# A fused RWKV attention, Fourier mixing and MLP kernel: another written-out order of the same operations, and an empty GpSimd instruction behind the transfers that GpSimd issues

## The chip, the core and the metric

The kernel runs on one core of a Trainium2 chip. The metric is the device time of one execution in microseconds (us); three runs of the kernel before gave 171.8, 172.41 and 172.97, so the median is 172.41 us. The engines are PE (TensorE, the matrix engine), DVE (VectorE), ACT (ScalarE), POOL (GpSimd) and SP (SyncE, which here only issues transfers). Each engine runs its own instructions strictly in the order in which the program lists them.

## The reference

Inputs are r, k and v of shape (4, 8, 768, 48): 4 batches, 8 heads, 768 steps, 48 channels a head; w and u of shape (8, 48); and two MLP weights, 384 x 1536 and 1536 x 384. All are float32, as is the output (4, 768, 384).

```
for t in range(768):                       # linear attention with decay w and bonus u
    cur   = u*k[t] (outer) v[t]
    y[t]  = r[t] @ (state + cur)
    state = w*state + k[t] (outer) v[t]
x   = y with the 8 heads side by side      # (4, 768, 384)
mix = real(fft over 768 steps of fft over 384 channels of x)
u2  = x + mix
un  = (u2 - mean) / sqrt(var + 1e-6)       # over the 384 channels
out = u2 + relu(un @ w_ch1) @ w_ch2
```

## The kernel before, in words

The 768 steps of each batch are cut into 6 chunks of 128, so there are 24 chunks, numbered 0 to 23 (0 to 5 are batch 0). For each chunk:

- `load` fetches k, r and v (192 KB each) through SP's queue (three of chunk 0 through ACT's) into rings of 6 buffers.
- `attend` scales k and r by powers of w into KR (L397, L400; DVE or POOL), transposes KR on PE (L421) and copies the result to KRT (L431 ACT, L432 DVE), or lets a DMA transpose it (L427). It multiplies KRT's halves into PR (L443, L445), makes the scores on PE (L455), masks them into MA (DVE straight from PSUM, L467; or an ACT copy AC, L462, and then POOL, L464), updates the state (L486, L499, L501), spreads the bonus into TT (L534), and sums the output X of the chunk (L546, L554, L556).
- `narrow` (batch 0, chunk by chunk) and `fold` (batches 1 to 3) add and subtract halves of X into HH and XF (L569, L572, L578 for batch 0). `fourier` does the two transforms as matmuls with tables (L647, L688), with TT and TR between them (L655, L656, L666, L669), adds x (UF, L700, L703), normalises (UB, L707 to L712; `st`, L718 or L719; `rstd`, L753), and transposes UB into UNT either on PE (L732, copied by L738 or L739) or by DMA (L758).
- `mlp1` and `mlp2` are the two MLP layers for each half batch (L776 with the ReLU in L781 or L782; L797 with L807). The outputs leave through POOL (L810) or SP (L811); the last 128 rows are cut in two (`finish`, L823 to L833).

Each output row block of 128 is worked on as soon as its inputs are there, so attention of later batches runs beside the MLP of earlier ones. The first MLP matmuls are those of half batch 1 (rows 384 to 767 of batch 0); what is written hp/1/ft below is layer 1 of that half, block ft. They need all three UNT blocks of that half and W1, which POOL fetches in two transfers of 576 KB (L851), called W1/0 and W1/1.

What sets the order is no loop. All operations are registered with a number, and with alternatives (which engine does it, or which way); the string `ORDER` lists some 1,410 of them as `number` or `number.alternative`, and `_Schedule.emit` emits them in this order. Buffers of a ring are handed out in it too. An engine's queue is thus the list's own operations in the list's order. `IDLES` registers matmuls on zeros (L283, `idle`), and `still` (L377) others; the list takes some of them.

POOL has one rule of its own, `chain`: each of its compute instructions carries a wait on the semaphore of the compute instruction before it. Transfers that POOL issues are outside the chain.

Of the kernel before, what the change touches and what calls it, by code (L numbers as in the profile page):

```python
# [61 lines left out]
class _Schedule:  # L62


    def __init__(self):
        self.ops, self.rings = [], {}
# [8 lines left out]
    def emit(self, order):  # L75
        last = {}
# [5 lines left out]
        for k, (n, a) in enumerate(order):  # L82
            o = self.ops[n]
            for t in o["new"]:
                ends = held[t.ring]
                m = min(range(len(ends)), key=ends.__getitem__)
                assert ends[m] < k, (o["name"], t.ring)
                ends[m] = last[t]
                t.value = self.rings[t.ring][m] if t.view is None else t.view(self.rings[t.ring][m])
            eng, key, fn = o["alts"][a]  # L90
            if fn is not None:
                made = fn()
                if eng == "POOL" and not key.startswith("dma"):
                    self.chain(made)
# [77 lines left out]
def kernel(  # L172
# [11 lines left out]
    nc = tc.nc  # L184
# [5 lines left out]
    hid_c = nc.inline_tensor(hid_n, name="hid_c")  # L190

    sch = _Schedule()
    before = []

    def chain(made):
        if before:
# [696 lines left out]
```

## Time and profile before

| what | value |
|---|---|
| runs (three) | 171.8, 172.41, 172.97 us |
| the profiled execution's own time | 173.32 us |
| its span, first to last instruction | 171.6 us |
| PE, DVE, ACT, POOL busy | 156.2, 127.8, 109.7, 92.3 us |
| instructions | 4305 |
| bytes moved by DMA | 27.08 MB, mean 158 GB/s |

The span is what the rows cover; 1.72 us of the execution lie around it. Busy times are unions of an engine's instructions. An engine that follows PE closely can be busy most of the time and yet wait for nothing that matters, so the stretches have to be read apart.

### The profile page before, as it was taken

To read this page: it belongs to the slowest core of one execution; us is meant where nothing else is said; L and a number is where in the kernel's file an instruction comes from. 1 tells how busy PE (TensorE), PEld (TensorE's weight loads), DVE (VectorE), ACT (ScalarE), POOL (GpSimd) and SP (SyncE) were. 2 spreads that over 40 slices of the span, in tenths; PEclk is the share of its full clock that TensorE was granted. 3 is DMA by queue.
4 is the path that set the end of the run, shared out by engine and by line. 5 is a ranking of instruction groups with operands and counts; after the bars stand their busy time and mean duration, and the time that the engine had idled before them with its cause. 6 is when DMAs were issued, how large, how long until landed. Compare 5 with 4: busy or idle time off the path is not lost.

```text
span 171.6 us, 4305 instructions
## 1 busy us (share of the span) xinstructions
PE 156.2 (91%) x1591; PEld 111.5 (65%) x1591; DVE 127.8 (74%) x310; ACT 109.7 (64%) x259; POOL 92.3 (54%) x128
## 2 busy tenths in 40 slices
PE   6179588999699999999999999999999999999991
PEld 1058466878477666867767687667766876766670
DVE  5298999899678959897867978988986984532241
ACT  2767898879578885765595676978634454562400
POOL 7548687799658142989774036578965221000021
PEclk9999978999999999999999999999999999999998
DMA  5999999899898999999989989999210217300223
GB/s 116 209 209 199 194 217 254 195 166 203 165 205 155 199 171 149 236 169 160 250 154 252 208 175 232 238 155 259 79 48 0 104 43 132 138 4 0 92 81 102
DMA packets 97879, 27.08 MB, mean 158 GB/s; under 512 B 94370, under 2 KB 96547, under 8 KB 97859
## 3 DMA queue, kind: packets, MB, share of 16 engines
q1 hardware_dynamic: 92480, 21.11, 68.4%
q0 software_dynamic: 2256, 5.12, 12.6%
q10 hardware_dynamic: 3122, 0.59, 2.1%
q8 instruction: 12, 0.20, 0.5%
q14 instruction: 9, 0.07, 0.1%
HBM read 19.77 MB, written 4.72 MB: 143 GB/s over the span
## 4 chain that ended last, share of the span: by engine, by line
PE 58%; DMA 12%; POOL 11%; DVE 6%; issue 6%; ACT 4%; POOLq 0%; DVEq 0%; ACTq 0%
PE bank L776 24%; PE bank L797 21%; DMA W<-in_moe_w_ch_dram 6%; POOL KR L397 3%; DMA wuc<-in_w_dram 3%; DMA KRT<-KR 3%; PE bank L647 2%; PE bank L688 2%; PE bank L455 2%; POOL MA L464 2%; PE bank L546 2%; POOL UB L712 1%; DVE TT L534 1%; PE bank L823 1%; POOL PR L443 1%
## 5 line engine op out<-in xcount | busy, mean ns | idle before, releaser
L776 PE MATMUL bank<-UNT,W 128*128 128x384 bf16 x288 | 54.3, 326 | 1.7 <-DMA W<-in_moe_w_ch_dram 1.3
L797 PE MATMUL bank<-W,HT 128*128 128x384 bf16 x276 | 52.3, 326 | 0.0
L781 ACT ACTIVATE HT<-bank 128x384 bf16<-128x384 f32 x73 | 33.1, 495 | 29.0 <-PE bank L776 28.8
L776 PEld LDWEIGHTS <-W 128*128 128x128 bf16 x288 | 31.1, 114 | 14.2 <-DMA W<-in_moe_w_ch_dram 1.5
L797 PEld LDWEIGHTS <-HT 128*128 128x128 bf16 x276 | 25.5, 97 | 14.2
L464 POOL TENSOR_SCALAR_AFFINE_SELECT MA<-AC 128x512 bf16<-128x512 bf16 x31 | 21.4, 690 | 14.3 <-issue 6.9
L810 POOL DMA_DIRECT2D out_dram<-osb x14 | 8.0, 571 | 28.2 <-DVE rstd L753 18.1
L397 POOL TENSOR_TENSOR KR<-kr,wtab 128x384 bf16<-128x384 f32 x17 | 19.1, 1124 | 6.8 <-ACT wtab L337 4.1
L462 ACT CAST AC<-bank 128x512 bf16<-128x512 f32 x31 | 17.7, 593 | 6.2 <-PE bank L455 2.8
L807 DVE SCALAR_TENSOR_TENSOR osb<-bank,rstd,UF 128x384 f32<-128x384 f32 x23 | 13.6, 612 | 7.8 <-PE bank L797 7.7
L782 DVE TENSOR_SCALAR HT<-bank 128x384 bf16<-128x384 f32 x23 | 12.3, 551 | 7.9 <-PE bank L776 5.9
L397 DVE TENSOR_TENSOR KR<-kr,wtab 128x384 bf16<-128x384 f32 x25 | 17.0, 697 | 1.3 <-DMA kr<-in_r_dram 1.3
L421 PE MATMUL bank<-ident,KR 128*128 128x128 bf16 x112 | 11.7, 252 | 4.8 <-DVE KR L400 3.7
L719 ACT ACTIVATE tn_t<-UF,sm 128x384 bf16<-128x384 f32 x21 | 13.1, 623 | 1.2 <-DVE UF L700 1.1
L421 PEld LDWEIGHTS <-KR 128*128 128x128 bf16 x112 | 8.8, 113 | 7.5 <-DVE KR L400 4.9
L534 DVE TENSOR_TENSOR TT<-V,bank 128x384 bf16<-128x384 bf16 x21 | 11.4, 548 | 2.7 <-ACT AC L462 1.2
L455 PE MATMUL bank<-KRT 64*128 64x128 bf16 x192 | 10.2, 229 | 2.0 <-ACT KRT L431 0.6
L554 DVE TENSOR_TENSOR X<-bank,TT 128x384 bf16<-128x384 f32 x17 | 9.2, 552 | 3.7 <-PE bank L546 3.6
L467 DVE TENSOR_TENSOR MA<-bank,mtri 128x512 bf16<-128x512 f32 x17 | 11.4, 682 | 0.6 <-PE bank L455 0.6
L647 PE MATMUL bank<-te_t,XF 128*128 128x193 bf16 x108 | 11.7, 247 | 0.0
L443 POOL TENSOR_TENSOR PR<-KRT 128x512 bf16<-128x512 bf16 x9 | 10.4, 1155 | 1.7 <-DMA KRT<-KR 1.1
L700 DVE SCALAR_TENSOR_TENSOR UF<-bank,X 128x384 f32<-128x384 f32 x21 | 11.0, 549 | 0.1
(112 smaller groups left out, 258.1 us busy)
## 6 DMA issues: line engine op xcount, KB each, us to landing
kr<-in_k_dram SPq DMA_DIRECT2D x23, 192.0 KB, 4.0
kr<-in_r_dram SPq DMA_DIRECT2D x23, 192.0 KB, 4.2
vt<-in_v_dram SPq DMA_DIRECT2D x23, 192.0 KB, 4.1
out_dram<-osb POOLq DMA_DIRECT2D x14, 192.0 KB, 3.3
out_dram<-osb SPq DMA_DIRECT2D x9, 192.0 KB, 2.6
W<-in_moe_w_ch_dram POOLq DMA_DIRECT2D x2, 576.0 KB, 9.2
W<-in_moe_w_ch_dram POOLq DMA_DIRECT2D x3, 384.0 KB, 7.1
te_t<-te_c SPq DMA_DIRECT2D x1, 579.0 KB, 5.0
```

Source lines behind the costliest of these rows:

```text
L397: return eng.tensor_tensor(out=o, in0=x, in1=y, op=AluOp.mult)
L421: nc.tensor.transpose(tps[s]()[:, p, :], KR()[:, s, p, :], ident)
L455: nc.tensor.matmul(A_ps[a]()[:, p, :], lhsT=KRT()[rows, 0, p, :], rhs=QT(p, rows), start=(p == 0), stop=(p == NP - 1), skip_group_check=True)
L462: op(("AC", i, a), [("ACT", "AC", lambda: nc.scalar.copy(AC(), A_ps[a]())), ("NONE", "", None)], r=[("A", i)], w=[("AC", i, a)], new=[AC], ...
L464: op(("MA", i, a), [("POOL", "MA", lambda: nc.gpsimd.affine_select(out=MA[a](), in_=AC(), pattern=[[0, NP], [1, 128]], base=0, channel_mul ...
L534: return eng.tensor_tensor(out=TT(), in0=V(), in1=x.unsqueeze(2).to_broadcast([128, H, D]), op=AluOp.mult)
L647: nc.tensor.matmul(fp()[:, par, :], lhsT=lhsT[:, g * CH:g * CH + 128], rhs=rhs, start=(nb == 0 and par == 0), stop=(nb == last and par == ...
L719: ("ACT", "SQ", lambda: nc.scalar.activation(out=squares, in_=UF()[:, j, :], func=Act.Square, scale=-float(DM), bias=sm()[:, j:j + 1], acc ...
L776: nc.tensor.matmul(hp(), lhsT=W1[:, dt, ft // 4 * 512 + ft % 4:(ft // 4 + 1) * 512:4], rhs=UNT()[:, :, dt, :], start=(dt == 0), stop=(dt = ...
L781: op(("HT", hf, ft), [("ACT", "HT", lambda: nc.scalar.activation(out=HT()[:, ft, :], in_=hp(), func=Act.Relu, scale=-1.0)), ("DVE", "HT", ...
L797: nc.tensor.matmul(mo(), lhsT=HT()[:, ft, j * 128:(j + 1) * 128], rhs=W2[:, ft, :], start=(ft == 0), stop=(ft == 11))
L807: one(("osb", hf, j), "DVE", "osb", lambda: nc.vector.scalar_tensor_tensor(out=osb(), in0=mo(), scalar=rstd()[:, j:j + 1], in1=UF()[:, j, ...
```

## The change

It is made of two parts.

First, `ORDER` is another list. It holds 1,414 entries of the same registered operations (before 1,413). Apart from the idle matmuls the operations are the same; their order and many of their alternatives differ. Decoded, the kinds that move most, by engine, with before -> after:

| kind (line) | DVE | POOL | ACT |
|---|---|---|---|
| scale k or r alone (L397) | 25 -> 26 | 17 -> 12 | |
| scale both at once (L400) | 3 -> 5 | | |
| PR (L443; L445 from PSUM) | 10 -> 15; 5 -> 3 | 9 -> 6 | |
| MA (L467; L464 with AC, L462) | 17 -> 22 | 31 -> 26 | 31 -> 26 |
| TT (L534; with DE, L530) | 21 -> 17 | 3 -> 7 | 3 -> 7 |
| KRT copies (L431, L432) | 13 -> 11 | | 15 -> 17 |
| HH, batch 0 (L569; L572 from PSUM) | 7 -> 4; 2 -> 6 | 3 -> 2 | |
| XF, batch 0 (L578) | 7 -> 11 | 5 -> 1 | |
| HH, other batches (L605) | 10 -> 12 | 2 -> 0 | |
| TR (L666, L669) | 2 -> 4 | 3 -> 1 | 3 -> 3 |
| UF (L700, L703) | 21 -> 23 | | 3 -> 1 |
| UB (L709, L712, L707) | 2 -> 4 | 11 -> 9 | 11 -> 11 |
| variance (L718 + L724; L719) | 3 -> 0 | | 21 -> 24 |
| ReLU of layer 1 (L782, L781) | 23 -> 27 | | 73 -> 69 |
| outputs issued (L810; SP: 11 -> 9) | | 14 -> 16 | |

On PE the idle matmuls go from 7 of 512 columns and 3 of 384 to 5 and 6, and matmuls that add x (L697) from 3 to 1. The DMA transposes stay 10 for KRT and 7 for UNT.

Places in the two lists that the prediction speaks of:

- W1 on POOL's queue. Before: the steps of XF for chunks 3 and 5 with W1/0 (1308) and W1/1 (1309) between them, then the rest. After: HH of chunk 5 (478.1), W1/1, PR of chunk 7 (522), W1/0, then V of chunk 8. PR of chunk 7 needs the copy KRT/7/1 (521), which is on DVE's queue.
- UNT of half batch 1: before two of its three copies from PSUM are DVE's (1080.3 and 1084.3), after one (1082.2).
- SP's queue behind r of chunk 12. Before: v/8, k/10, k/11, r/11, r/10, v/9, v/10, k/15 and then the transposing transfer UNT/0/0 (1057.4). After: UNT/0/0 stands right behind r/12, and v/10, k/15, k/13, k/11, r/11 and more behind it.
- ACT's second table load, `sqrttab` (192): before between X of chunk 2 and S of chunk 5, in the first quarter; after behind the first MLP half batches, ahead of the first square root (1048). `tn` (273) moves from DVE to ACT.

Second, `chain` puts an empty instruction on POOL ahead of the first compute instruction that follows one or more transfers issued by POOL, and the wait of that compute instruction is on the empty one. In the new list this gives 12 empty instructions, ahead of: icol_i, WD0/0, PR/7, V/8, MA/10/1, KR/17/1, V/14, MA/16/0, V/20, UB/2/2, KR/22/0 and TR/3/0.

```diff
-        self.ops, self.rings = [], {}
+        self.ops, self.rings, self.issued = [], {}, False
...
             if fn is not None:
-                made = fn()
-                if eng == "POOL" and not key.startswith("dma"):
-                    self.chain(made)
+                if eng != "POOL":
+                    fn()
+                elif key.startswith("dma"):
+                    fn()
+                    self.issued = True
+                else:
+                    self.chain(fn, self.issued)
+                    self.issued = False
...
 ORDER = """
-155 159 152 202 30 203 150 158 151 168 208 172 205 206 154 211 209 173 164 199.1 163 165 200.1 181.1 179 162 161 201.1
...
-1308 1011 516 490 477 1021 1022 1017 496 1018 559 1003 478 503.1 479.1 1309 495 522.2 575.2 504 1004 1023 480 1005
...
+152 159 158 9 150 151 177 202 208 168 153 199.1 200 209 205 206 160 155 180 203 182 183 211 175 154 156 157 163 204
...
+1002 1009 451 478.1 480 546.2 479 547.2 235 1010 1021 1022 520.1 575.1 503.1 1309 228 236 606.3 1003 1023 579 577 1014
+1015 1016 1017 580 1004 1005 518.1 521.1 1018 1024 1006 1025 1026 494.1 1019 495.1 1011 1012 522.1 516 528 1020.1 1027
+523 490 1308 550.1 1013 1028 549.2 524 578 504 581 1030 508.1 532 1029 1058 548.2 552.1 1064 553.1 535.1 1070 1031
...
-    before = []
-
-    def chain(made):
-        if before:
-            tc.add_manual_dep(made.ins, before[-1].ins.name,
+    last = []
+
+    def chain(fn, issued):
+        if issued:
+            last.append(nc.gpsimd.engine_nop())
+        made = fn()
+        if last:
+            tc.add_manual_dep(made.ins, last[-1].ins.name,
...
-        before.append(made)
+        last.append(made)
```

## Rows read from the trace of the kernel before

**Rows 1.** stretches: PE, PEld, DVE, ACT, POOL busy; clock; DMA share; GB/s

```profile
7.40:42.90 35.50, 30.04 (x423) 24.05 (x423) 32.87 (x81) 29.17 (x68) 26.64 (x32) 0.95 1.08 204
42.90:44.70 1.80, 0.43 (x6) 0.12 (x2) 1.28 (x4) 1.16 (x4) 1.61 (x3) 1.00 1.00 196
44.70:135.00 90.30, 89.80 (x936) 64.05 (x937) 74.80 (x168) 61.41 (x151) 54.43 (x70) 1.00 0.96 170
135.00:165.00 30.00, 30.00 (x204) 20.43 (x202) 14.65 (x42) 14.02 (x34) 3.38 (x6) 1.00 0.25 73
165.00:171.60 6.60, 2.79 (x27) 2.10 (x24) 1.96 (x4) 0.00 (x0) 1.08 (x2) 0.88 0.34 119
```

**Rows 2.** timeline of PE: start us, length us, line, operation, [idle before <-releaser]

```profile
43.06 0.33 PE L776 MATMUL bank<-UNT,W 128*128 128x384 bf16 x1
44.70 1.49 PE L776 MATMUL bank<-UNT,W 128*128 128x384 bf16 x8 [1.31 <-DMA W<-in_moe_w_ch_dram]
```

**Rows 3.** chain that ended last: start us, length us, what

```profile
34.40 10.25 DMA W<-in_moe_w_ch_dram
...
140.46 3.90 PE bank L797 x24
```

**Rows 4.** transfers: tensors, queue, count, KB, median us from issue to landing

```profile
W<-in_moe_w_ch_dram POOLq DMA_DIRECT2D x2, 576.0 KB, 9.2
W<-in_moe_w_ch_dram POOLq DMA_DIRECT2D x3, 384.0 KB, 7.1
te_t<-te_c SPq DMA_DIRECT2D x1, 579.0 KB, 5.0
```

**Rows 5.** timeline of DVE

```profile
7.46 1.83 DVE L400 TENSOR_TENSOR KR<-kr,wtab 128x768 bf16<-128x768 f32 x2 [4.29 <-ACT wtab L337]
...
10.80 1.01 DVE L397 TENSOR_TENSOR KR<-kr,wtab 128x384 bf16<-128x384 f32 x2
...
18.91 0.42 DVE L443 TENSOR_TENSOR PR<-KRT 128x512 bf16<-128x512 bf16 x1
...
23.68 1.18 DVE L443 TENSOR_TENSOR PR<-KRT 128x512 bf16<-128x512 bf16 x1
...
36.65 0.59 DVE L656 CAST TT<-bank 97x386 bf16<-97x386 f32 x1
...
42.56 0.36 DVE L739 COPY UNT<-bank 128x384 bf16<-128x384 bf16 x1 [0.36 <-ACT UNT L738]
```

**Rows 6.** DVE's groups, first 44 us; xcount, busy us, mean ns, idle before

```profile
L467 DVE TENSOR_TENSOR MA<-bank,mtri 128x512 bf16<-128x512 f32 x10 | 6.7, 679 | 0.0
L397 DVE TENSOR_TENSOR KR<-kr,wtab 128x384 bf16<-128x384 f32 x8 | 5.5, 708 | 0.0
L534 DVE TENSOR_TENSOR TT<-V,bank 128x384 bf16<-128x384 bf16 x8 | 4.3, 545 | 0.3 <-PE bank L519 0.3
L432 DVE COPY KRT<-bank 128x512 bf16<-128x512 bf16 x10 | 4.0, 405 | 0.4 <-PE bank L421 0.4
...
L569 DVE TENSOR_TENSOR HH<-X 128x192 bf16<-128x192 bf16 x7 | 2.2, 332 | 0.2 <-ACT X L556 0.2
L578 DVE TENSOR_TENSOR XF<-HH 128x196 bf16<-128x196 bf16 x7 | 1.7, 259 | 0.8 <-POOL XF L578 0.7
L700 DVE SCALAR_TENSOR_TENSOR UF<-bank,X 128x384 f32<-128x384 f32 x3 | 1.6, 540 | 0.0
```

**Rows 7.** timeline of POOL

```profile
0.92 0.12 POOL L299 IOTA icol_i<- 128x3 int32 x1 [0.41 <-POOLq L877]
...
38.43 1.16 POOL L443 TENSOR_TENSOR PR<-KRT 128x512 bf16<-128x512 bf16 x1
...
69.48 0.60 POOL L810 DMA_DIRECT2D out_dram<-osb  x1
70.11 1.02 POOL L397 TENSOR_TENSOR KR<-kr,wtab 128x384 bf16<-128x384 f32 x1
71.19 0.83 POOL L666 COPY TR<-TT 97x768 bf16<-97x768 bf16 x1
```

118 rows, old and new, of the table ORDER are left out of this document.

## The prediction

> **What bounds the kernel now.** I read the busy time by stretch first. From 44.70 to 165 us PE is busy 89.80 of 90.30 and 30.00 of 30.00 us; in the 35.5 us before 42.9 it is busy 30.04 [rows 1], and that flatters it, since ends of matmuls are modelled. DVE is the full engine of that early stretch (32.87 of 35.50), POOL (26.64) and ACT (29.17) are less so. So the time is: how long it takes until the MLP can feed PE without a break, plus the PE work left then, plus the gaps after it, plus a tail.
>
> The timeline of PE shows where the break-free part begins: one layer-1 matmul at 43.06, then 1.31 us idle, then eight in a row from 44.70, released by W's transfer [rows 2]. In the chain of waits that transfer runs 10.25 us from 34.40 and is the second of the two halves of W1 [rows 3]. By the list the first block, hp/1/0, needs only W1/0, so in effect the first MLP block waits for both halves, whichever is asked for first. DVE's last UNT copy starts at 42.56 and ends at 42.92 [rows 5], so data and weights were 1.8 us apart.
>
> The tail is 6.60 us from 165 with 2.79 of PE [rows 1]: last matmuls, a final DVE step, a transfer, the end of the program. All else after 44.70 is PE work at its pace: 24 matmuls of 384 columns in 3.90 us, 0.1625 each [rows 3].
>
> **The change, part by part.** The sum is made against the profiled execution, 173.32 us (span 171.6 and 1.72 around it), which is 0.91 above the median of 172.41.
>
> *When UNT is ready.* I count, in both lists, what DVE has to do from the first scaling to the last UNT copy of half batch 1, and price the differences by their rows [rows 6]: three more single scalings (3 x 0.708 = 2.1), two UF (1.1), four XF (1.0), one HH (0.3) and two TR, priced as the KRT copy (2 x 0.405 = 0.8); three TT fewer (-1.6), two MA (-1.4), one KRT copy (-0.4). That is +1.9; other kinds differ by an instruction or two, with one copy (0.4) fewer on balance: +1.5. Both begin when chunk 0's first inputs and decay table are there, 7.46 [rows 5]. With as many waits as before UNT is ready at 42.92 + 1.5 = 44.4; DVE idled 35.50 - 32.87 = 2.6 us in this stretch, so with none at 41.8. I take the middle, 43.1, since the new list takes ACT's table load out of this stretch and gives POOL less to do, which feed DVE, but not all waits go.
>
> At one place a rule speaks to this term. Two free scalings take 1.01 us [rows 5], 0.51 each, against a mean of 0.708 [rows 6]; PR takes 0.42 at one time and 1.18 at another [rows 5], where POOL scales beside it. The eight scalings thus lost 8 x 0.2 = 1.6 us. The Trainium skill (SBUF — State Buffer, Who interferes with whom) says that a DVE instruction with two SBUF inputs and a GpSimd instruction that reads SBUF exclude each other, and that whoever is issued first blocks the other entirely. By the rows' means the sum is as above; by the rule the loss would shrink with POOL's own scalings (three instead of eight ahead of this point), making UNT about 1.0 us earlier, and POOL's turn to be blocked would grow. I keep the means.
>
> *When W1 is there.* Before, both halves are asked for within 1.3 us of each other. After, the second request (W1/0) stands on POOL's queue behind PR of chunk 7, which waits for DVE's copy KRT/7/1. Counted at the same prices, that copy has as much DVE work ahead of it as the copy at 36.65 had before [rows 5], so it ends at 37.1 with as many waits, 34.5 with none. PR takes 1.16 on POOL [rows 7], so the request goes out between 35.7 and 38.3. A half of W1 landed 9.2 us after its issue in the median and the second after 10.25; a table of the same size, 579 KB, took 5.0, and 384 KB of W2 7.1 [rows 3, 4]. The other bound is 5.0, the table's. The lists say which is nearer: SP's queue now has UNT/0/0 right behind r/12, and the loads behind it can't start before that, so W1/0 shares with few loads. I take the mean of 5.0 and 7.1: 37.0 + 6.1 = 43.1, within 40.7 and 48.6. The later of two times near 43.1 I put at 43.5: **-1.2 us** against 44.70.
>
> *PE work left.* Ahead of the first layer-1 matmul the new list has 0.55 us less PE work by columns (two 512-column idles, two sets of transposes and two additions of x fewer; three 384-column idles and a state update more). The whole list has 0.27 less. So 0.28 more is left, and 0.16 for the matmul that before got in at 43.06: **+0.4**.
>
> *Gaps after that.* Over the whole lists DVE has more (MA +5, PR +5, ReLU +4, XF and HH; TT, KRT and variance less): 7 to 8 us by the same kind of count, of which 1.5 lie ahead of the first block. In 44.70 to 135 DVE idled 90.30 - 74.80 = 15.5 us [rows 1], which covers 6 if the pauses fall right. Gap cost: nothing if all is covered and -0.5 if the old gap of 0.50 goes too, +6 if none is; nearest is the row of the stretch itself, 83% busy with 0.50 of gap, so I take **+0.3**.
>
> *The empty instructions.* Twelve. No row shows one. A compute instruction behind a transfer began 0.03 after its end (69.48 + 0.60 to 70.11), one behind another compute 0.06 after (71.13 to 71.19); a POOL instruction with next to no work, the iota, takes 0.12 [rows 7]. So 0 to 0.2 each, 2.4 in all; they compute nothing, so there is no gain. They are nearest to the iota. Behind each waits the next POOL step and what reads it. POOL is idle 36 of the 90 us [rows 1], which hides eight; four lie earlier, and of these only the one ahead of PR/7 is on W1's way (0.1, within the bounds above). **0.**
>
> *Moved with one answer.* ACT's table load and the `tn` step move along an ACT that had 6.3 us free before 42.9; loads behind UNT/0/0 on SP serve chunks 10 on, whose use is later in the list; the last output keeps SP and the one before it goes to POOL, ahead of it. No cost; if the loads come late, KR of chunk 11 is next to wait.
>
> Sum: -1.2 + 0.4 + 0.3 = -0.5, so 172.8 by the profile and **171.9** at the median.
>
> **The rivals.** (A measurement tells about 1% from no change, 1.7 us.)
>
> *The start gains in full.* DVE's waits vanish and W1/0 takes the table's 5.0: UNT 41.8, W1 40.7, first block at 42.0: -2.7 + 0.4, and no new gap: 170.1. For it: less POOL work beside DVE, the table load gone from the start. Against: DVE was 93% busy with 1.5 us less to do. Chance 0.32, with what lies below it.
>
> *W1/0 comes late.* Slower, by one wait: PR/7 holds the request back to 38.3, and the landing takes the second half's 10.25: 48.6, +3.9 + 0.4: 176.7. It decides from a landing at 46.0 on (1% in the sum). For it: two requests that stood 1.3 us apart now stand apart by a DVE copy and a PR. Against: the quiet SP queue. Chance 0.14, for any landing past that point.
>
> *DVE becomes the bound in the middle.* If some 2.5 of the 6 added us find no pause, +2.5 with -1.2 + 0.4 gives 174.1; with 3.5, 175.1. For it: pauses of an in-order queue are not where the work is. Against: PE lost 0.50 with DVE at 83%. Chance of over 1%: 0.12.
>
> *The change does nothing*: the empty instructions vanish in the build, and the order comes to the same limits: 172.4. It is part of "within 1%"; alone 0.03.
>
> **How the numbers follow.** Forecast case (within 1%, 170.7 to 174.1, its own range) 0.42 with the last rival in it; faster 0.32; slower 0.14 + 0.12 = 0.26. The range takes in the fast rival's 170.1 and a little below, and the slower ones up to 175.1, which leaves out the late W1's far end: 169.6 to 175.2.
>
> **What would show it.** In the changed profile: the start of the unbroken layer-1 matmuls (43.5; right between 42 and 45) and its releaser, W or UNT; the issue of the second W1 transfer (37.0) and its landing; DVE's share of 44.70 to 135 (about 90%) with PE's idle time there (0.8); POOL's starts behind transfers 0.1 to 0.2 later than the transfers' ends. Wrong would be: a first block past 46, PE idle over 2 us in the middle, or a POOL chain of waits on the critical path.

## The result and the profile after

The changed kernel took 175.11 us in the median of 16 runs (172.83 to 176.76), the kernel before 172.63 beside it (16 runs). The ratio is 1.0107, with an interval of 1.0072 to 1.0142: slower by about 1%, where 171.9 was forecast. The ratios here leave out executions over 1.5% above the fastest of their kernel (four of the changed kernel's 16, the profiled one of 176.39 us among them) and the medians don't, so the profile shown has this kernel's loss at its larger end.

The lines of the changed kernel stand 8 further down than before (L776 is L784, L397 is L405). First the stretches, with the columns of [rows 1] (length; PE, PEld, DVE, ACT, POOL busy; granted clock; DMA share; GB/s), cut where the changed kernel's stages lie:

```profile
7.40:41.20 33.80, 28.77 (x415) 22.09 (x415) 30.93 (x88) 27.53 (x65) 19.35 (x26) 1.00 1.10 207
41.20:44.10 2.90, 0.01 (x1) 0.04 (x2) 1.14 (x3) 2.87 (x8) 2.04 (x4) 0.77 1.21 229
44.10:50.60 6.50, 6.50 (x29) 3.68 (x30) 2.67 (x6) 2.01 (x6) 0.48 (x1) 0.58 0.99 190
50.60:135.00 84.40, 83.75 (x888) 59.27 (x886) 76.62 (x169) 59.77 (x143) 42.67 (x53) 1.00 0.87 167
135.00:165.00 30.00, 30.00 (x211) 20.94 (x210) 16.74 (x41) 13.02 (x34) 5.32 (x9) 1.00 0.26 73
165.00:174.70 9.70, 5.55 (x45) 3.84 (x43) 2.69 (x5) 0.00 (x0) 1.62 (x3) 1.00 0.23 81
```

The early work is done sooner (33.80 us from 7.40 on, 35.50 before) and the middle is as full as before. What is new is the third row: PE is busy all of its 6.50 us, but at a granted clock of 0.58. Busy time alone would call that stretch perfect. By the microsecond:

```profile
43.00:44.00 1.00, 0.00 (x0) 0.00 (x0) 0.00 (x0) 0.97 (x4) 0.86 (x3) 0.50 1.28 258
44.00:45.00 1.00, 0.91 (x3) 0.44 (x4) 0.00 (x0) 0.86 (x4) 0.58 (x1) 0.50 0.53 107
...
48.00:49.00 1.00, 1.00 (x4) 0.44 (x3) 0.94 (x3) 0.02 (x1) 0.00 (x0) 0.50 1.16 232
49.00:50.00 1.00, 1.00 (x6) 0.54 (x5) 0.84 (x2) 1.00 (x3) 0.00 (x0) 0.70 1.01 198
50.00:51.00 1.00, 1.00 (x14) 0.75 (x13) 0.17 (x1) 0.24 (x1) 0.00 (x0) 1.00 1.12 226
```

0.50 is the lower of the two levels, 1.2 of 2.4 GHz. It was granted from 42.77 us, while PE stood idle, to 49.60, and so for most of the first layer-1 blocks. In the kernel before, each microsecond from 42 to 51 shows 1.00. PE's timeline (as [rows 2]):

```profile
40.83 0.36 PE L554 MATMUL bank<-V,MA 128*128 128x48 bf16 x8
44.09 1.12 PE L784 MATMUL bank<-UNT,W 128*128 128x384 bf16 x3 [2.90 <-DMA W<-in_moe_w_ch_dram]
45.01 0.63 PE L429 MATMUL bank<-ident,KR 128*128 128x128 bf16 x4
45.44 2.12 PE L784 MATMUL bank<-UNT,W 128*128 128x384 bf16 x6
47.35 0.63 PE L429 MATMUL bank<-ident,KR 128*128 128x128 bf16 x4
47.78 3.01 PE L784 MATMUL bank<-UNT,W 128*128 128x384 bf16 x12
50.63 0.36 PE L554 MATMUL bank<-V,MA 128*128 128x48 bf16 x8
50.83 1.15 PE L784 MATMUL bank<-UNT,W 128*128 128x384 bf16 x6
```

Compare the two groups of six: start to the next group's start is 1.91 us at 45.44 (47.35 - 45.44) and 0.99 at 50.83 (the next row begins at 51.82). The first block began 0.61 us earlier than before (44.09 against 44.70), after 2.90 us of idle PE instead of 1.31. The releaser is W again, and the chain of waits (as [rows 3]) names the second of the two requests again, which is now W1/0. (The first block of the new list, hp/1/10, uses columns of W1/1 alone, which landed at 38.67; it waited for W1/0 all the same. No run tests why.) The second line is a late row for the pace of a matmul:

```profile
34.72 9.23 DMA W<-in_moe_w_ch_dram
...
141.76 4.88 PE bank L805 x30
```

There a matmul is back at 4.88 / 30 = 0.163 us. DVE until UNT is ready (groups to 40.15 us, as [rows 6]):

```profile
L405 DVE TENSOR_TENSOR KR<-kr,wtab 128x384 bf16<-128x384 f32 x11 | 5.9, 551 | 2.9 <-DMA kr<-in_k_dram 2.0 <-DMA kr<-in_r_dram 0.9
L475 DVE TENSOR_TENSOR MA<-bank,mtri 128x512 bf16<-128x512 f32 x7 | 4.5, 668 | 0.0
...
L542 DVE TENSOR_TENSOR TT<-V,bank 128x384 bf16<-128x384 bf16 x5 | 2.7, 548 | 0.9 <-ACT V L421 0.9
```

and its timeline, first scalings and last UNT copy (as [rows 5]):

```profile
5.33 0.56 DVE L405 TENSOR_TENSOR KR<-kr,wtab 128x384 bf16<-128x384 f32 x1 [1.96 <-DMA kr<-in_k_dram]
6.79 0.56 DVE L405 TENSOR_TENSOR KR<-kr,wtab 128x384 bf16<-128x384 f32 x1 [0.90 <-DMA kr<-in_r_dram]
...
39.77 0.36 DVE L747 COPY UNT<-bank 128x384 bf16<-128x384 bf16 x1
```

UNT of half batch 1 is complete at 40.13, and before at 42.92. POOL's timeline around the second W1 request (as [rows 7]):

```profile
33.62 1.15 POOL L451 TENSOR_TENSOR PR<-KRT 128x512 bf16<-128x512 bf16 x1 [1.56 <-DVE KRT L440]
34.72 0.85 POOL L859 DMA_DIRECT2D W<-in_moe_w_ch_dram  x1
35.67 0.50 POOL L422 CAST V<-vt 128x384 bf16<-128x384 f32 x1
```

### The profile page after: what moved, and what is told of

It is laid out like the page before. It is cut to its first block, busy times and chain, and to the rows that moved or that the text cites. A ratio compares the mean times of both kernels' runs of the same rounds, so it can differ in the third digit from the quotient of the medians.

```text
span 174.7 us, 4301 instructions
## 1 busy us (share of the span) xinstructions
PE 158.0 (90%) x1590; PEld 110.9 (64%) x1590; DVE 134.3 (77%) x329; ACT 109.9 (63%) x261; POOL 75.8 (43%) x107
## 4 chain that ended last, share of the span: by engine, by line
PE 57%; DVE 14%; issue 13%; DMA 8%; POOL 3%; ACT 2%; POOLq 0%; DVEq 0%; ACTq 0%
PE bank L784 21%; PE bank L805 16%; DMA W<-in_moe_w_ch_dram 5%; PE bank L696 3%; PE bank L655 3%; PE bank L429 3%; PE bank L463 3%; DVE KR L405 3%; DMA wuc<-in_w_dram 2%; PE bank L554 2%; DVE MA L475 2%; PE bank L494 2%; POOL out_dram L818 1%; DVE XF L622 1%; PE bank L533 1%
## 5 line engine op out<-in xcount | busy, mean ns | idle before, releaser
L784 PE MATMUL bank<-UNT,W 128*128 128x384 bf16 x288 | 57.1, 336 | 2.9 <-DMA W<-in_moe_w_ch_dram 2.9
L784 PEld LDWEIGHTS <-W 128*128 128x128 bf16 x288 | 31.1, 116 | 16.0 <-issue 4.7
L790 DVE TENSOR_SCALAR HT<-bank 128x384 bf16<-128x384 f32 x27 | 14.4, 551 | 12.4 <-PE bank L784 11.4
L472 POOL TENSOR_SCALAR_AFFINE_SELECT MA<-AC 128x512 bf16<-128x512 bf16 x26 | 17.4, 671 | 13.3 <-ACT AC L470 9.4
L470 ACT CAST AC<-bank 128x512 bf16<-128x512 f32 x26 | 14.6, 587 | 6.3 <-PE bank L463 4.7
L405 DVE TENSOR_TENSOR KR<-kr,wtab 128x384 bf16<-128x384 f32 x26 | 15.1, 600 | 2.9 <-DMA kr<-in_k_dram 2.0
L475 DVE TENSOR_TENSOR MA<-bank,mtri 128x512 bf16<-128x512 f32 x22 | 14.5, 678 | 0.6 <-PE bank L463 0.4
L405 POOL TENSOR_TENSOR KR<-kr,wtab 128x384 bf16<-128x384 f32 x12 | 12.2, 1021 | 1.1
L663 ACT CAST TT<-bank 97x386 bf16<-97x386 f32 x11 | 6.3, 603 | 9.6 <-PE bank L655 9.6
L451 POOL TENSOR_TENSOR PR<-KRT 128x512 bf16<-128x512 bf16 x6 | 6.9, 1156 | 11.2 <-ACT tn_t L727 9.0
L439 ACT COPY KRT<-bank 128x512 bf16<-128x512 bf16 x17 | 9.8, 594 | 2.9 <-PE bank L429 2.8
L655 PEld LDWEIGHTS <-XF 128*128 128x128 bf16 x120 | 10.1, 97 | 1.2 <-issue 0.3
```

Source lines behind the costliest of these rows:

```text
L405: return eng.tensor_tensor(out=o, in0=x, in1=y, op=AluOp.mult)
L470: op(("AC", i, a), [("ACT", "AC", lambda: nc.scalar.copy(AC(), A_ps[a]())), ("NONE", "", None)], r=[("A", i)], w=[("AC", i, a)], new=[AC], ...
L472: op(("MA", i, a), [("POOL", "MA", lambda: nc.gpsimd.affine_select(out=MA[a](), in_=AC(), pattern=[[0, NP], [1, 128]], base=0, channel_mul ...
L475: ("DVE", "MA", lambda: nc.vector.tensor_tensor(out=MA[a](), in0=A_ps[a](), in1=mtri.unsqueeze(1).to_broadcast([128, NP, 128]), op=AluOp.m ...
L655: nc.tensor.matmul(fp()[:, par, :], lhsT=lhsT[:, g * CH:g * CH + 128], rhs=rhs, start=(nb == 0 and par == 0), stop=(nb == last and par == ...
L784: nc.tensor.matmul(hp(), lhsT=W1[:, dt, ft // 4 * 512 + ft % 4:(ft // 4 + 1) * 512:4], rhs=UNT()[:, :, dt, :], start=(dt == 0), stop=(dt = ...
```

## The experiments

Theories. **C**: what costs is the granted clock, which falls in or right behind PE's wait for W1/0. **N**: the empty instructions cost. **D**: DVE is the bound in the middle of the kernel. **W** (later called L): the transfer engines are full from 30 to 46 us, so a transfer lands when what was asked for ahead of it has been moved, whoever asks. **I**, in the later runs: only idle time itself counts, not the clock. All ratios are to the kernel before on the same chip. Each trace is of one execution.

**e1: the changed order without empty instructions.**

```diff
     def chain(fn, issued):
-        if issued:
-            last.append(nc.gpsimd.engine_nop())
         made = fn()
```

> The changed order alone: chain as before, no empty instruction. Theory C (clock): PE waits 2.9 us for the second half of W1 (41.2 to 44.1), its granted clock then falls to half, and the first MLP blocks run at half pace up to 49.6 us, which costs 2 to 2.8 us; the empty instructions cost nothing. It expects the time of the changed kernel, 175.1 within 0.6, and the same fall of the clock near 43 us. Theory N (empty instructions): 12 of them, some 0.1 us each where POOL is late, make 1.2 us or more; it expects 173.9 or less. Theory D (DVE in the middle) expects 175.1 too.

Measured 174.71, ratio 1.0088 [1.0053, 1.0122]. The loss stays, and so does the wait, with three matmuls at half pace behind it; the clock was at 0.50 from 43.08 to 46.49 us, half as long as in the changed kernel's profile:

```profile
42.96 1.04 PE L782 MATMUL bank<-UNT,W 128*128 128x384 bf16 x3 [1.99 <-DMA W<-in_moe_w_ch_dram]
...
48.49 0.36 PE L552 MATMUL bank<-V,MA 128*128 128x48 bf16 x8
```

**e2: the order before, with empty instructions.** The changed kernel with the `ORDER` of before.

```diff
     def chain(fn, issued):
+        if issued:
+            last.append(nc.gpsimd.engine_nop())
```

> The order before with the empty instructions behind POOL's transfers. Theories C and D: the time of the kernel before, 172.6 within 0.6; first unbroken layer-1 matmuls near 44.7. Theory N: 1.2 us or more slower, 173.8 and up.

Measured 172.97, ratio 1.0012 [0.9977, 1.0046]. N falls by both runs. In e2's profiled execution (174.61 us) PE happened to wait 1.86 us for W1, and there, too, the clock stood at 0.50 from 46 to 48 us, so the fall does not need the new list:

```profile
45.25 2.63 PE L784 MATMUL bank<-UNT,W 128*128 128x384 bf16 x8 [1.86 <-DMA W<-in_moe_w_ch_dram]
```

```profile
46.00:48.00 2.00, 2.00 (x10) 0.80 (x10) 1.02 (x2) 0.49 (x1) 0.09 (x1) 0.50 1.06 210
```

**e3: both requests for W1 side by side.**

```diff
-... 503.1 1309 228 236 606.3 ... 523 490 1308 550.1
+... 503.1 1309 1308 228 236 606.3 ... 523 490 550.1
```

> The changed kernel with one entry of the list moved: W1/0 is asked for right behind W1/1, ahead of PR of chunk 7. Theory C: request at 32.1 instead of 34.7, both halves landed by 41.5, PE's wait under 1 us, clock at its full level from 30 us on; start of the MLP 41.2 to 42.0 (2.1 to 2.9 earlier) and the half-clock stretch gone (2 to 2.8): 170.2, between 169.4 and 171.0. Theory D (the loss is DVE's in the middle, the start does not matter beyond its own shift): 172.2 to 173.0, the shift alone. Theory W (the transfer engines are the limit, and an earlier request lands no earlier): 174.5 or more.

Measured 172.93, ratio 1.0005 [0.9979, 1.0032]; the 170.2 of theory C was missed, and the time alone is what theory D expected (172.2 to 173.0). PE's timeline:

```profile
42.16 0.65 PE L784 MATMUL bank<-UNT,W 128*128 128x384 bf16 x3
44.26 0.40 PE L429 MATMUL bank<-ident,KR 128*128 128x128 bf16 x4 [1.45 <-POOL KR L405]
44.49 1.14 PE L784 MATMUL bank<-UNT,W 128*128 128x384 bf16 x6
```

The clock stayed at 1.00 and the 2.2 us of the median came back. But W1/0, asked for 2.38 us earlier (32.34), landed only 1.94 earlier (42.02), and r of chunk 10, asked for at 32.40, landed at 43.65 instead of 40.10: the wait for W became one for KR of chunk 10. So W holds as well: moving W1 up pushes something else back.

**e4: PE kept running through the wait.** Twelve 512-column matmuls on zeros ahead of the first block.

```diff
-... 586 544 1375 607.3
+... 586 544 100 101 102 103 104 105 106 107 108 109 110 111 1375 607.3
```

> The changed kernel with 12 idle matmuls of 512 columns (12 x 0.22 = 2.6 us) put ahead of the first layer-1 block, so that PE works while it waits for W1. Everything else, the late W1/0 too, stays. Theory C: the first block still starts at 44.0 to 44.5, but the clock stays at its full level; 2 to 2.8 us come off: 172.7, between 172.2 and 173.3. Theories D and N: no gain, 175.1 within 0.6, or up to 0.5 more.

Measured 173.87, ratio 1.0079 [1.0051, 1.0106]: by the medians 1.2 less than the changed kernel, where 2.4 were expected; by the ratios (1.0079 against 1.0107) 0.3%, with intervals that overlap. The gain in time is thus not clear by this run alone. PE's timeline, then the clock:

```profile
42.16 3.04 PE L292 MATMUL bank<-zero 128*128 128x512 bf16 x12
45.04 0.65 PE L785 MATMUL bank<-UNT,W 128*128 128x384 bf16 x3
...
48.90 0.36 PE L555 MATMUL bank<-V,MA 128*128 128x48 bf16 x8
```

```profile
42.00:45.00 3.00, 2.92 (x23) 1.34 (x21) 1.47 (x3) 2.97 (x8) 2.22 (x3) 1.00 1.07 203
45.00:49.00 4.00, 4.00 (x34) 2.88 (x33) 2.67 (x6) 2.23 (x7) 0.64 (x1) 1.00 1.00 189
```

From the first block to the L555 behind 21 matmuls of layer 1 it takes 3.86 us (48.90 - 45.04); the changed kernel needed 6.54 for the same instructions (50.63 - 44.09). That is 2.68 us for the clock in that execution. In e1's, with the shorter stretch at 0.50, the same instructions took 5.53 (48.49 - 42.96), so there the price was 1.67. Part of the expected gain went into a later start (45.04 against 44.09): in this execution W1/0 was asked for at 35.84 and landed at 44.78, and the zeros ran 0.26 past it.

**e6, e7: the order before, with W1/1 one POOL step later, without and with ten matmuls on zeros.**

```diff
-... 479.1 1309 495 522.2
+... 479.1 495 1309 522.2
-... 1085.3 1355 1357 ...                 (e7)
+... 1085.3 100 101 ... 109 1355 1357 ...  (e7)
```

> The kernel before, with the second request for W1 (W1/1) moved one POOL step back, behind MA/6/0: request about 36.2 instead of 34.40. The transfers are busy throughout 30 to 46 us, so W1/1 should land near 46.2 and PE, which has its data at 43.4, idle some 2.8 us there (before: 1.31). Theory C (the granted clock falls to its lower level when PE has idled through such a wait, and the first layer-1 matmuls then run at half pace for some us, worth about 2.2): a granted clock of 0.5 somewhere in 44 to 51 us, and the time is the wait's own 1.5 plus 2.2 above before: about 176.2. Rival I (only the idle time itself counts, the changed list's loss lies elsewhere): 174.0, matmuls of 0.163 us from the start. If W1/1 lands as early as before: 172.5 by both.

> As the run before it, with ten 512-column matmuls on zeros ahead of hp/1/0, which keep PE running through most of the wait (they add no result). Theory C: the same landing of W1/1, no fall of the clock, and about 2.2 us less than without the ten matmuls: 174.0. Rival I: no difference, 174.0 against 174.0, or up to 0.3 slower.

Measured 172.87 (1.0004 [0.9968, 1.0040]) and 173.91 (1.0058 [1.0030, 1.0086]). The pair didn't make its wait: asked for at 35.20 instead of 34.40, W1/1 landed at 44.29 instead of 44.65, and PE idled 0.95 with the clock at 1.00. So it doesn't tell C from I. It fits W once more, and shows that matmuls on zeros without a long wait to fill cost about a microsecond.

**e8, e9: e3 with layer-1 blocks 8 and 9 ahead of chunk 10's transposes; e9 also with the loads of v/9, k/12 and r/12 behind UNT/0/0.**

```diff
-... 1375 607.3 610.3 1052.4 ... 612.3 1371 613.3 567.1 1373 1034.1
+... 1375 607.3 1371 1373 610.3 1052.4 ... 612.3 613.3 567.1 1034.1
-... 235 ... 1309 1308 228 236 606.3 ... 1057.4 231   (e9)
+... 1309 1308 606.3 ... 1057.4 228 235 236 231       (e9)
```

> The changed kernel with both requests for W1 side by side (as e3) and layer-1 blocks 8 and 9 ahead of the transposes of chunk 10, whose KR came 1.45 us late in e3. Nine instead of three matmuls then stand ahead of that wait, 0.98 us more. If the wait for KR/10 was what kept e3 at the time of before: 1.0 us faster than e3, 171.7 to 171.9, clock full. If PE only meets the next late loads (the transfers are the limit): no change, 172.6 to 172.9.

> As e8, and the loads of v of chunk 9 and k and r of chunk 12 (576 KB) stand behind UNT/0/0 on SP's queue, so they start after 41 us. At about 200 GB/s they took 2.9 us of the transfer engines between 33 and 46 us. If the transfers are the limit: W1/0 lands by 41.3 (e3: 42.02), k and r of chunk 10 by 42.3 (43.65), no wait of over 0.5 us at 42 to 46, the clock full, and 170.8 to 171.5, faster than both kernels. If a transfer's share is what was asked for first and later loads don't matter: W1/0 still at 42.0 and 171.8. If chunk 9's or 12's inputs are then late: a wait of PE at 46 to 52 and 172.5 or more.

e8: median 173.5 (171.02 to 175.71), ratio 0.9980 [0.9937, 1.0022]. No gain that can be told, against 1.0 expected: in the profiled execution W1/0 landed at 43.42, and PE waited 1.12 for it instead of for KR. e9: 173.4, ratio 1.0041 [1.0009, 1.0072]. Its trace is of an execution of 179.95 us, which a wait later in the kernel (3.35 us, ending at 65.12) helps to make long; it is read here up to 50 us only. With 576 KB fewer behind it W1/0 still landed at 43.05 (41.3 expected), so what is asked for later hardly matters here; what is left is what was asked for ahead or beside it (hid, which is the table of the second transform, and k and r of chunk 10). KR of a later chunk then came 0.87 us late (PE, 49.29).

**e10, e11: the order before with a real wait; W1/1 behind PR of chunk 8, without and with twelve matmuls on zeros.**

```diff
-... 479.1 1309 495 ... 555.1 524.1 525.1
+... 479.1 495 ... 555.1 1309 524.1 525.1
-... 1085.3 1355 1357 ...                 (e11)
+... 1085.3 100 101 ... 111 1355 1357 ...  (e11)
```

> The kernel before, with the second request for W1 behind PR of chunk 8 on POOL: request about 39.6 instead of 34.40 (in e6, at 35.20, it still landed at 44.29, since the transfers ahead of it set that). With all loads of 33 to 36 us ahead of it, it should land near 46.3, and PE idle 2.5 to 3 us, as in the changed kernel. Theory C (PE's idling through the wait lowers the granted clock): 0.5 in part of 44 to 51 us; the later start 1.6 plus about 2.2 for the clock, 176.4. Rival I (only the idle time counts): 174.2, matmuls of 0.163 us from the start. No wait at all (landing by 44.7 again): 172.6.

> The same with twelve 512-column matmuls on zeros ahead of hp/1/0 (2.6 us of PE in the wait; they add no result). Theory C: the same landing, clock full from 40 us on, 174.3, that is 2.1 less than without the twelve. Rival I: no less than without them, 174.2 against 174.2.

Measured 176.70 (1.0221 [1.0175, 1.0268]) and 175.26 (1.0149 [1.0112, 1.0186]). e10, PE's timeline, then its clock by stretch:

```profile
46.19 2.75 PE L776 MATMUL bank<-UNT,W 128*128 128x384 bf16 x8 [1.89 <-DMA W<-in_moe_w_ch_dram]
...
53.71 0.36 PE L546 MATMUL bank<-V,MA 128*128 128x48 bf16 x8
```

```profile
44.00:46.00 2.00, 0.30 (x1) 0.05 (x1) 1.08 (x3) 1.00 (x2) 1.72 (x4) 0.76 1.15 204
46.00:48.00 2.00, 1.81 (x6) 0.91 (x7) 0.00 (x0) 0.49 (x1) 1.08 (x3) 0.50 1.26 248
48.00:50.00 2.00, 2.00 (x20) 1.07 (x19) 1.07 (x3) 0.43 (x1) 1.35 (x2) 0.50 1.18 221
50.00:52.00 2.00, 2.00 (x8) 0.92 (x7) 1.44 (x3) 0.66 (x3) 0.00 (x0) 0.54 1.06 203
```

e11, PE's timeline:

```profile
44.16 2.76 PE L284 MATMUL bank<-zero 128*128 128x512 bf16 x11
46.76 1.63 PE L777 MATMUL bank<-UNT,W 128*128 128x384 bf16 x9
...
51.83 0.36 PE L547 MATMUL bank<-V,MA 128*128 128x48 bf16 x8
```

W1/1 landed at 46.14 and 46.53, so the wait is nearly the same. From the first block to the same L546 step it takes 7.52 us in e10 and 5.07 in e11, whose clock is 1.00 from 42 to 54 us (one more layer-1 matmul is in e11's figure, since e10 got one in ahead of the wait). The clock's price in the order before is thus at least 2.45 by these two traces. By I, e11 would not have been faster; it is, by 1.44 in the median (2.1 were expected) and by 0.7% in the ratio, although it starts 0.57 later and carries more matmuls. The mean granted clock was 0.999 or 1.0 in all six executions of e11 and 0.968 to 0.99 in all six of e10. Filling the wait kept the clock up, and that paid.

**e12, e13: e8 with both requests ahead of HH of chunk 5; e13 also with hid ahead of r of chunk 8.**

```diff
-... 449.2 466 475 ... 503.1 1309 1308 228
+... 449.2 466 1309 1308 475 ... 503.1 228
-... 222 224 342.1 272 369.1 ...   (e13)
+... 222 272 224 342.1 369.1 ...   (e13)
```

> As e8, with both requests for W1 ahead of HH of chunk 5 on POOL: 28.4 and 29.2 instead of 31.7 and 32.6. Theory L (a transfer lands when what was asked for before it has been moved, about 200 KB a us): W1/0 lands by 40, but hid, asked for at 31.3, lands near 39 instead of 35.3, and the second transform that needs it starts 3 us late: 174 to 175.5. Rival (hid on SP's queue gets its share beside W1): hid by 36.5, first block at 42.3 without a wait, 171.3.

> As e12, with hid ahead of r of chunk 8 on SP's queue, request about 28.7 instead of 31.3, into the stretch of 30 to 32 us where the transfers moved only 107 to 123 GB/s in e9, e3 and the changed kernel. By theory L hid lands by 34, W1/0 by 40.5, r of chunk 8 near 37 instead of 34.5: first block at 42.3 without a wait, clock full, 170.8 to 171.6, faster than both kernels. If r of chunk 8 is then what the attention waits for: 172.5 or more.

Measured 178.69 (1.0266 [1.0198, 1.0335]) and 177.64 (no ratio; 173.96 to 179.3). L was right that hid is pushed back (landed at 40.26 in e12, 39 expected). Both times came out above what was expected; the new wait also drew the clock down, which the expectations had not priced, but how much of the excess that is was not measured. e12, PE and then its clock:

```profile
40.30 0.82 PE L696 MATMUL bank<-hid_t,TT 97*128 97x192 bf16 x4 [5.03 <-DMA hid_t<-hid_c]
```

```profile
36.00:40.00 4.00, 0.00 (x0) 0.00 (x0) 0.00 (x0) 0.07 (x1) 0.47 (x1) 0.62 1.15 256
40.00:42.00 2.00, 1.70 (x10) 1.46 (x11) 0.84 (x3) 0.51 (x2) 1.24 (x3) 0.50 0.83 163
```

In e13 PE idled 6.49 us, for V of an early chunk whose load, asked for at 28.41 behind W1/1, landed at 39.90: hid had not gone out sooner than 30.31. No version beat both kernels.

## Why the prediction was wrong, step by step

*The step that failed* is the one that treated the wait for W1 as costing its own length and nothing else. The sum had no term for the pace of PE behind a wait. That term is 2.68 us in the profiled execution (6.54 against e4's 3.86) and 1.67 in e1's; either turns the forecast's -0.5 into a loss. By the profiled executions: start -0.61, PE work left +0.4 as counted from the lists, clock +2.68, gaps in the middle +0.15 (84.40 - 83.75 = 0.65 against 0.50), and 0.3 between PE's last matmul and the end (4.10 against 3.79). That is 2.9; the executions differ by 176.39 - 173.32 = 3.07. The medians differ by less, 175.11 - 172.63 = 2.48. The changed kernel's own runs point the same way: the two of its 16 with a mean granted clock of 1.00 took 172.83 and 172.95, the other 14, at 0.98 to 0.99, 174.06 to 176.76. A mean doesn't tell where in the kernel the clock was low, and of the 16 only one has a trace; executions without the fall may also have waited less.

The warning stood in the first row of the first group: a clock of 0.95 in 7.4 to 42.9 us [rows 1]. (There the clock was at 0.50 from 23.24 to 26.66.) It was read past, because DVE was the full engine there and PE's pace was taken to cost nothing.

*When UNT is ready* was wrong, too, by 3.0 us: 43.1 forecast, 40.13 in the trace, outside its bounds of 41.8 to 44.4. (In the traces of e1, e3, e4, e8 and e9, which have the same early order but for the moved entries, it was ready between 39.99 and 41.45: part of the 3.0 is scatter, but all lie below the bounds.) DVE's waits stayed as they were (32.73 - 29.99 = 2.74 us from 7.40 to 40.13, against 2.6), but its work fell by 2.9 instead of growing by 1.5. The kinds I counted came out as counted where their price held (TT -1.6; MA -1.5, from nine of 6.0 us up to 42.95). Two errors can be put into numbers. Two of the scalings ran ahead of 7.40, at 5.33 and 6.79, as chunk 0's inputs were waited for one by one (1.1 us). And the scalings took 551 ns instead of 708 (11 x 0.157 = 1.7). The rule of the Trainium skill that the prediction weighed and set aside (SBUF — State Buffer, Who interferes with whom) spoke for that: the loss to POOL's own scalings shrank as POOL had fewer. It would have given 1.0; the trace gives 1.7 and does not show the mechanism itself. The earlier start of 5.33 was not counted at all. The other 1.6 us of the 4.4 lie in smaller kinds that I had put at -0.4 together; the traces show most of it as one sum of X fewer (0.56), `tn` gone to ACT (0.46) and the two WD copies at 0.51 instead of 0.96.

This error is what made the wait. Data and weights were forecast for the same moment, 43.1; in fact the data came 3 us sooner and the weights 0.9 later. Faster early work made PE's idle time longer (2.90 against 1.31), not the start much earlier. The forecast for the start, 43.5, was near (44.09), and in the range called right, while the time was wrong. That nearness is luck, and so is it that 175.11 lies just inside the range of 169.6 to 175.2: its upper end came from DVE as the bound in the middle, which the trace doesn't show.

*When W1 is there*: request 34.72 (37.0 forecast, and 1.0 below the bounds of 35.7 to 38.3), landing 43.96 (43.1; within bounds). The two errors nearly cancel: the request came early with DVE, and the transfer took 9.23 instead of 6.1. The mean of 5.0 and 7.1 was taken because SP's queue looked quiet; the transfers' share was 1.10 to 1.21 through this stretch, and e3, e6, e9 and e12 fit a landing that goes by the bytes ahead. [Rows 3, 4] had it: 10.25 and 9.2 for this very transfer.

*Gaps in the middle*: +0.15 measured, +0.3 forecast; DVE 76.62 of 84.40 = 91%, about 90% forecast. D was no bound. *Empty instructions*: POOL's step behind the transfer starts 0.10 after its end (35.57 to 35.67), 0.03 before [rows 7], within the 0 to 0.2; no cost that e1 and e2 can tell. *Moved things*: no late load on the path in the changed kernel; the KR of chunk 10 came up only when W1 was moved (e3).

*The rivals*: "W1/0 comes late" was to decide from a landing at 46.0 on. It decided at 43.96, since it is the wait in front of the landing that has the price, not the landing. Its size was the wrong measure.

The Trainium skill has this behaviour (TensorE: Matmul & The Clock Gate, HAM oscillation — how this bites in real kernels): in its example, matmuls behind waits of about 3 to 5 us for a transfer start at the lower level. The trace agrees, with 0.50 at 43 to 49 us behind 2.90 of idle PE, and in e2 a wait of 1.86 was enough. The same page (Part 1) puts the price of a ramp from the lower level below 1% of a typical kernel's span; here it is 2.68 of 174.7, or 1.5%, in the changed kernel's trace and 1.67 of 173.0, or 1.0%, in e1's, and the measurement decides.

What stays open: e13 and e9 leave the best order of the early loads unknown. Why one execution has the longer stretch at 0.50 and another the shorter is not shown. No kernel was run that makes UNT later in the changed order, so that the earlier data lengthen the wait is read from the traces alone.

## What to carry to other kernels

Where an idle time of PE precedes a dense run of matmuls, ask whether the granted clock falls in it, and price the matmuls behind it at the lower level in the cases where it may. A stage that gets its data earlier while its weights can't come earlier only lengthens that wait; look at the later of the two, and at what else the full transfer engines carry, before counting a gain. Read the clock column of a stretch beside the busy column, above all where PE shows 100%.

## What the runs showed of the hardware that was not expected

- Behind waits of PE of 1.86 (e2), 1.89 (e10), 1.99 (e1), 2.90 (the changed kernel), 3.35 (e9, at 65.12, for ACT), 5.03 (e12) and 6.49 us (e13) the granted clock went to 0.50 within the wait or up to 0.2 us behind its end, and the next matmuls ran at that level; behind 0.95 (e6), 1.12 (e8), 1.31 (before) and 1.45 us (e3) it was 1.00 in the profiled execution.
- A long wait is not the only way there: in the kernel before the clock was at 0.50 from 23.24 to 26.66 us, with PE busy throughout and no wait above 1.10 us in the 10 us ahead of it.
- At 0.50 a group of six 384-column matmuls took 1.91 us where it took 0.99 at 1.00, and the lower level lasted to about 46.5 in e1 and 49.6 in the changed kernel, with PE busy without a break since 42.96 and 44.09.
- Two requests for W1 0.8 us apart landed 3.4 to 4.5 us apart (38.54 and 43.05 in e9, 35.49 and 38.86 in e12), and a load asked for beside them, r of chunk 10, took 11.38 us in e9 where the median of its kind is 4.3.
